# A 640-point forward transform split by residues modulo five, one slab at a time, with its output columns placed in order in PSUM

## The chip, the cores and the metric

The kernel runs on one core of one Trainium2 chip. The metric is device microseconds of one execution, the median of three runs. A core has five engines with a queue each: TensorE (PE in the profile, its weight loads PEld), VectorE (DVE), ScalarE (ACT), GpSimd (POOL) and SyncE (SP), which here issues all DMAs. Each queue runs its instructions in the order in which the program emits them, and an instruction waits until what it reads is written and what it overwrites has been read. SBUF is the working memory, PSUM (eight banks of 512 fp32 values per partition) is where TensorE writes.

## The reference, cut to what matters

`x` is 2048 x 640 in bf16. Two branches start from the same row-normalized `xn`: a spectral filter `s` and a gated feed-forward network `g`.

```python
xn = _layernorm(x, axis=-1)
X = jnp.fft.rfft2(xn, axes=(-2, -1)) * (w_r + 1j * w_i)      # 2048 x 321
s = jnp.fft.irfft2(X, s=(2048, 640), axes=(-2, -1))
g = _silu((_gelu(xn @ w_gate) * (xn @ w_up)) @ w_down)       # 640 -> 1536 -> 640
return x + s * g
```

## The kernel before

The 2048 rows are held as 16 *slabs* of 128 rows (row = 16 * partition + slab). Slabs 4g to 4g+3 form *group* g of the feed-forward network (FFN), 512 rows.

**The order of work** is one hand-written list, `back` (L787 to L801), of 144 *steps* of FFN work; `plan` (filled by `put(step, item)`) names what else is emitted directly after each step. So the order on every queue is fixed by this list: after a step's FFN instructions come its plan items, in the order of the `put` calls. Steps 3 to 15 are small FFN pieces of group 0; from step 16 an *FFN half* is five matmuls of 512 columns, for `w_gate` (even steps, `psg`, evicted by ScalarE's gelu at L726) or `w_up` (odd steps, `psu`, evicted by VectorE's product at L728 into `uT`). Steps 24 to 35 are the twelve thirds of group 0's down projection (eight matmuls of 320 columns each, L747), 36 to 59 the halves of group 1, 60 to 71 its down projection, 72 to 107 group 2, 108 to 143 group 3. `psg` and `psu` have two banks each.

**The spectral branch** lies between these steps.

- Normalization of a slab: statistics on VectorE (L182, L187), the root on POOL (`root`, L198), and either `norm` on VectorE (L204) or `norm_act` on ScalarE (L435, with `shift` on POOL for its bias).
- *Folds* on VectorE, for two slabs at once: `fold_a` (L444, L445) forms x[d] + x[d+320] and x[d] - x[d+320], `fold_b` (L453, L454) adds and subtracts mirrored halves of each. That splits the 640-point transform into four products of 160 inputs and up to 161 outputs.
- `slab_S1` (L483): the first factor of the 2048-point transform, five matmuls of 128 columns per slab into `pz`; ScalarE copies `pz` to SBUF (L485).
- `group_D` (L503): the 640-point products, for one slab and then five times three. `d_group` (L487) does 128 of the 160 inputs by L493 and the other 32, four row groups of the array side by side, by L497, for 161 columns each, into two PSUM tiles `pd`. Two copies (L509, two of the twelve on VectorE) interleave even and odd frequencies on their way to `zd` in SBUF, and SP stores `zd` to the DRAM scratch `ZDR`, two or four DMAs per group.
- `load_B2` reads `ZDR` back transposed (tile B, L534), `s2_in` and `s2_out` (L560 to L593) do the rest of the 2048-point transform and the filter, `UDR` and `load_V` turn it back.
- The inverse: `slab_S1i` (L639, copy L641), `group_Di` (`d_group` with the table `FI`, copies L664), `group_cs`, `group_Y` and `finish` on VectorE.

`pz`, `pd`, `px`, `pu` and `pv` all take turns in one ring of two PSUM tiles of two banks (`psB`, tag "b"); `group_D` and `group_Di` take both at once.

The step numbers of the stages: the forward stage is `F0 = 30` to `z_end` = 56; `s2` starts at `z_end + 9` = 65 and takes 24 steps, `load_V` comes at 89, the inverse starts at `vs0` = 97 with a new group of three slabs every 7.5 steps, its S1 at a, a+2 and a+4, its D at a+6.

`FT` and `FI` are the tables of the forward and the inverse 640-point products, made at the start: phases on ScalarE (`ft_v`), reduced on POOL (`ft_phase`), sines on ScalarE (`ft_sin`). GEN is one area of SBUF from which the tables' intermediate values are cut.

Of the kernel before, what the change touches and what calls it, by code (L numbers as in the profile page):

```python
# [76 lines left out]
def build(nc, env):  # L77
# [275 lines left out]

    mg = {}
# [80 lines left out]
        nc.scalar.activation(out=X[:, n1, :], in_=X[:, n1, :], func=ACT.Identity, scale=rstd[n1], bias=nmr[n1])  # L435
# [2 lines left out]
    uvs = {}

    def fold_a(pair):  # L440
        xn = X[:, 2 * pair:2 * pair + 2, :]
        assert ("n", 2 * pair + 1) in done
        uvs[pair] = uvt = work.tile([P, 2, D], BF16, tag="uv", bufs=2, name="uvt")
        nc.vector.tensor_tensor(out=uvt[:, :, 0:320], in0=xn[:, :, 0:320], in1=xn[:, :, 320:640], op=ALU.add)  # L444
        nc.vector.tensor_tensor(out=uvt[:, :, 320:640], in0=xn[:, :, 0:320], in1=xn[:, :, 320:640], op=ALU.subtract)  # L445

    def fold_b(pair):
        xf[pair] = f = work.tile([P, 2, D], BF16, tag="xf", bufs=2, name="f")
        s4 = uvs.pop(pair).rearrange("p k (t d) -> p k t d", t=2)
        dm = f[:, :, 0:512].rearrange("p k (g d) -> p k g d", g=4)  # L450
        dr = f[:, :, 512:640].rearrange("p k (g d) -> p k g d", g=4)
        for gs, op in ((slice(0, 4, 3), ALU.add), (slice(1, 3), ALU.subtract)):
            nc.vector.tensor_tensor(out=dm[:, :, gs, :], in0=s4[:, :, :, 32:160], in1=s4[:, :, :, 287:159:-1], op=op)  # L453
            nc.vector.tensor_tensor(out=dr[:, :, gs, :], in0=s4[:, :, :, 0:32], in1=s4[:, :, :, 319:287:-1], op=op)  # L454
# [22 lines left out]
    zbuf = fv.rearrange("p g l -> p (g l)").bitcast(BF16)[:, 0:4 * D].rearrange("p (s c k) -> p s c k", s=4, c=5)  # L477

    def slab_S1(n1):
        f = xf[n1 // 2]  # L480
        pz = psB.tile([P, 5, P], FP32, tag="b")
        for c in range(5):
            nc.tensor.matmul(pz[:, c, :], lhsT=chunk(f, n1 % 2, c), rhs=Tfwd[:, n1, :], start=True, stop=True)  # L483
# [1 line left out]
        nc.scalar.copy(out=Zt[n1], in_=pz)  # L485

# [10 lines left out]
                nc.tensor.matmul(out[a][g], lhsT=lhs[a][r, 4, :], rhs=T[r, 4, 0:w], start=False, stop=(a == n - 1))  # L497
# [4 lines left out]

    def group_D(i):  # L503
        n0, n = DF[i]
        pd = d_group([Zt.pop(n0 + a) for a in range(n)], FT, LH)
        zd = work.tile([P, 3, 2, LP], BF16, tag="zd", bufs=2, name="zd")[:, 0:n]
        for b in range(2):
            ev = nc.vector.tensor_copy if i in (2, 5) and b == 1 else nc.scalar.copy
            ev(out=zd.rearrange("p a c (m b) -> p a c m b", b=2)[:, :, :, :, b], in_=pd[b])  # L509
# [320 lines left out]
    put(17, stats, 8)  # L830
    put(19, stats, 9)
    put(23, fold_a, 0)
    for it in ((silu_table,), (tinv_sin, 0), (tinv_sin, 1), (ft_sin, 0)):
        put(23, *it)
    put(24, fold_b, 0)
    put(28, mg_mask)
    put(25, root, 8, 2)
    put(25, fold_a, 1)
    for q in range(4):
        put(24 + q, tfwd, q)  # L840
    put(27, norm, 8)
    put(28, fold_b, 1)
    put(29, stats, 10)
# [1 line left out]
    put(29, mg_sin)
    put(29, mg_build)
    put(31, norm, 9)
    put(32, stats, 11)
    put(33, root, 10, 2)
    put(34, norm, 10)  # L850
    put(35, norm, 11)
    put(38, stats, 12)
    put(41, stats, 13)
    put(41, root, 12, 2)
    put(42, stats, 14)
    put(43, norm, 12)
    put(44, norm, 13)
    put(44, stats, 15)
    put(45, root, 14, 2)
    put(46, norm, 14)  # L860
    put(47, norm, 15)
# [2 lines left out]
    for i, (n0, n) in enumerate(DF):
        a = F0 if i == 0 else F0 + 5 * i - 3
        for k in range(n):
            put(a + k, slab_S1, n0 + k)
        put(a + n, group_D, i)
    for pair in range(6):
        b = F0 + 3 * pair + (0 if pair < 4 else 3)  # L870
        put(b, fold_a, pair + 2)
        put(b + 1, fold_b, pair + 2)
    z_end = F0 + 26
# [88 lines left out]
```

## Time and profile before

| | us |
|---|---|
| median of three runs | 203.33 |
| lowest, highest | 203.01, 203.89 |
| the profiled execution, whole time | 203.86 |
| its span, first to last instruction | 201.7 |

| stretch of the span, us | what runs | PE busy | DVE busy | ACT busy | DMA share |
|---|---|---|---|---|---|
| 0.00 to 10.00 | start, slabs 0 and 1 | 8.27 | 7.77 | 3.71 | 0.87 |
| 26.70 to 35.40 | FFN halves 16 to 23 | 8.70 | 5.16 | 5.97 | 1.06 |
| 35.40 to 51.20 | steps 24 to 35 | 15.80 | 11.75 | 11.56 | 0.79 |
| 51.20 to 86.10 | steps 36 to 59 | 34.88 | 22.36 | 24.89 | 0.58 |
| 102.00 to 130.00 | steps 72 to 92, s2 | 28.00 | 15.60 | 21.19 | 0.31 |
| 150.60 to 183.00 | steps 108 to 131, inverse | 32.40 | 25.05 | 18.80 | 0.29 |

The first table's difference between whole time and span is what lies around the first and last instruction. The second is read across: an engine's busy time beside the length of the stretch. Rows of instructions further down read: start, duration (for several in a row, of all together), engine, line, operation, output <- input, shapes, count, and in square brackets how long the engine sat idle before and what released it. Rows of groups read: busy microseconds in all, mean nanoseconds of one, then the idle time before them and its releasers.

### The profile page before, as it was taken

What the parts mean: (1) busy time and instruction counts of PE and PEld (TensorE: products, weight loads), DVE (VectorE), ACT (ScalarE), POOL (GpSimd) and SP (SyncE); (2) the same over time, 40 slices, a digit from 0 to 9 for tenths busy, and PEclk for the clock granted to TensorE, in tenths of its full rate; (3) what the DMA queues carried; (4) which work ended last, traced back from release to release, by engine and by line L of the source; (5) the groups of instructions that cost most, each with busy time, mean ns of one, the idle gap of its engine ahead of it and who ended that gap; (6) DMA issues with size and microseconds to landing.
All of it is one profiled execution on the core that took longest, in us unless ns stands there. A gap on an engine that the chain in (4) does not pass through costs nothing.

```text
span 201.7 us, 4218 instructions
## 1 busy us (share of the span) xinstructions
PE 196.1 (97%) x1581; PEld 119.5 (59%) x1581; DVE 128.0 (63%) x339; ACT 122.7 (61%) x210; POOL 34.3 (17%) x61
## 2 busy tenths in 40 slices
PE   7899999999999999999999999999999999999993
PEld 5678854777555555576634334456775555556772
DVE  7786866677398972435566476223358776867673
ACT  2457657966886777414887878324475647476632
POOL 4327869972201100000000000000000000000000
PEclk9999999999999999999999999999999999999999
DMA  6999999958566647339844202389301343224312
GB/s 164 307 301 283 356 344 195 144 103 301 116 170 153 159 115 300 116 94 301 237 134 132 92 25 81 130 199 328 129 0 67 99 111 120 69 94 142 89 67 63
DMA packets 40163, 32.43 MB, mean 161 GB/s; under 512 B 14928, under 2 KB 38096, under 8 KB 39888
## 3 DMA queue, kind: packets, MB, share of 16 engines
q1 hardware_dynamic: 40144, 32.17, 56.9%
q8 instruction: 12, 0.20, 0.4%
q14 instruction: 7, 0.06, 0.1%
HBM read 19.03 MB, written 7.88 MB: 133 GB/s over the span
## 4 chain that ended last, share of the span: by engine, by line
PE 89%; DMA 4%; DVE 3%; SPq 1%; POOL 1%; issue 1%; ACT 0%
PE psu L722 24%; PE psg L722 24%; PE psg L747 13%; PE psu L747 13%; PE pd L493 5%; PE pv L639 2%; DMA Vin<-UDR 2%; PE pz L483 2%; PE pu L587 2%; DMA X<-in_A_x_dram 2%; PE pd L497 2%; PE px L560 2%; DVE st L182 1%; SPq L610 1%; POOL rst L198 1%
## 5 line engine op out<-in xcount | busy, mean ns | idle before, releaser
L722 PE MATMUL psu<-xnT,Wu 128*128 128x512 bf16 (+2 forms) x295 | 61.5, 340 | 0.3
L722 PE MATMUL psg<-xnT,Wg 128*128 128x512 bf16 (+2 forms) x295 | 61.4, 340 | 0.0
L728 DVE TENSOR_TENSOR uT<-psu,ge 128x512 bf16<-128x512 f32 (+2 forms) x59 | 34.3, 584 | 30.1 <-PE psu L722 22.5
L726 ACT ACTIVATE ge<-psg 128x512 bf16<-128x512 f32 (+2 forms) x59 | 30.5, 518 | 27.8 <-PE psg L722 25.9
L747 PEld LDWEIGHTS <-uT 128*128 128x128 bf16 x396 | 37.1, 98 | 14.3 <-issue 0.6
L722 PEld LDWEIGHTS <-Wu 128*128 128x128 bf16 x295 | 26.6, 98 | 23.1 <-issue 2.9
L722 PEld LDWEIGHTS <-Wg 128*128 128x128 bf16 x295 | 26.7, 98 | 21.8 <-issue 1.4
L747 PE MATMUL psg<-Wd,uT 128*128 128x320 bf16 (+1 forms) x204 | 30.4, 294 | 0.0
L747 PE MATMUL psu<-Wd,uT 128*128 128x320 bf16 (+1 forms) x192 | 29.2, 296 | 0.0
L572 DVE TENSOR_TENSOR X<-xs,W 128x972 bf16<-128x972 bf16 (+2 forms) x22 | 13.3, 648 | 10.2 <-ACT xs L568 10.2
L641 ACT CAST W<-pv 128x640 bf16<-128x640 f32 x16 | 11.1, 692 | 6.0 <-PE pv L639 6.0
L182 DVE BATCH_NORM_STATS2 st<-X 128x6 f32<-128x320 bf16 x32 | 14.2, 481 | 0.2 <-DMA X<-in_A_x_dram 0.2
L509 ACT CAST zd<-pd 128x966 bf16<-128x966 f32 (+1 forms) x10 | 10.5, 1103 | 5.3 <-PE pd L497 5.3
L664 ACT ACTIVATE W<-pd 128x960 bf16<-128x960 f32 (+2 forms) x14 | 10.1, 780 | 5.0 <-PE pd L497 5.0
L485 ACT CAST GEN<-pz 128x640 bf16<-128x640 f32 x16 | 11.0, 696 | 3.2 <-PE pz L483 3.2
L593 ACT CAST X<-pu 128x486 bf16<-128x486 f32 (+4 forms) x22 | 12.3, 558 | 0.4
L568 ACT CAST xs<-px 128x972 bf16<-128x972 f32 (+2 forms) x11 | 10.3, 937 | 2.1 <-PE px L560 2.1
L198 POOL TENSOR_TENSOR rst<-ve,mhalf 128x1 f32<-128x1 f32 (+2 forms) x9 | 6.5, 719 | 26.8 <-DVE ve L196 26.8
L670 DVE TENSOR_TENSOR W<-W 128x960 bf16<-128x960 bf16 (+1 forms) x12 | 6.8, 599 | 4.8 <-ACT W L664 4.8
L697 DVE TENSOR_TENSOR Yall<-Yall,G 128x640 bf16<-128x640 bf16 (+3 forms) x19 | 8.2, 434 | 1.6 <-ACT G L752 1.3
L756 DVE SCALAR_TENSOR_TENSOR G<-th,psu 128x320 bf16<-128x320 f32 x8 | 3.9, 488 | 8.2 <-ACT th L755 8.2
L698 DVE TENSOR_TENSOR Yall<-Yall,xt 128x640 bf16<-128x640 bf16 (+3 forms) x19 | 8.3, 439 | 0.7
(132 smaller groups left out, 197.4 us busy)
## 6 DMA issues: line engine op xcount, KB each, us to landing
W<-W SPq DMA_DIRECT2D x4, 642.0 KB, 4.2
xt<-in_A_x_dram SPq DMA_DIRECT2D x8, 320.0 KB, 3.8
ZDR<-zd SPq DMA_DIRECT2D x20, 120.4 KB, 3.2
UDR<-X SPq DMA_DIRECT2D x10, 240.8 KB, 2.2
out_dram<-Yall SPq DMA_DIRECT2D x14, 160.0 KB, 1.9
B<-ZDR SPq DMA_DIRECT2D x8, 240.8 KB, 3.9
W<-UDR SPq DMA_DIRECT2D x4, 481.5 KB, 7.3
X<-in_A_x_dram SPq DMA_DIRECT2D x3, 640.0 KB, 7.6
```

What stands on the lines that cost most here:

```text
L182: nc.vector.bn_stats(out=st[:, k, :], in_=X[:, n1, 320 * k:320 * k + 320])
L485: nc.scalar.copy(out=Zt[n1], in_=pz)
L509: ev(out=zd.rearrange("p a c (m b) -> p a c m b", b=2)[:, :, :, :, b], in_=pd[b])
L568: nc.scalar.copy(out=xs, in_=px[:, :, 0:n * w].rearrange("p k (h l) -> p k h l", l=w))
L572: nc.vector.tensor_tensor(out=pp[-1], in0=xs, in1=WT[:, :, h0:h0 + n, l0:l0 + w], op=ALU.mult)
L593: nc.scalar.copy(out=us[:, :, :, c0:c0 + (w + 1 - m) // 2], in_=pv[:, :, :, m:w:2])
L641: nc.scalar.copy(out=vs, in_=pv)
L664: nc.scalar.activation(out=eo[:, b, :, a0:a1].rearrange("p k a n -> p a k n"), in_=py[b][:, a0:a1], func=ACT.Copy, scale=(2.0 if silu[a0] ...
L722: nc.tensor.matmul(ps, lhsT=WT[:, c, t * P:(t + 1) * P], rhs=xnT[g][:, c, c0:c1_], start=(c == 0), stop=(c == 4))
L726: nc.scalar.activation(out=ges[t], in_=ps, func=ACT.Gelu_apprx_tanh)
L728: nc.vector.tensor_tensor(out=uT[g][:, t, c0:c1_], in0=ps, in1=ges[t], op=ALU.mult)
L747: nc.tensor.matmul(ph, lhsT=uT[g][:, t, j * P:(j + 1) * P], rhs=Wd[:, t, c0:c1_], start=(t == 0), stop=(t == NT - 1))
```

## The change

The 640-point forward product is split by the frequency's residue modulo five. The frequencies that are multiples of five need only the sum of the five blocks of 128 inputs (`fold_y`, result `y0`). For all others one block can be subtracted from the rest (`fold_x`), which leaves 512 inputs; `fold_a` and `fold_b` fold these by mirror images into four groups of 128. So every product has exactly 128 rows and there is no remainder of 32: `slab_D` does four matmuls of 128 columns and two of 65 for one slab, and `group_D` is gone for the forward stage. `l_cols` places each matmul's output columns at their frequency's own place in PSUM: steps of 2 and gaps for the four groups, steps of 5 for the multiples of five. One ScalarE copy of 2 x 321 dense columns per slab follows, and two stores to `ZDR` per slab (32 instead of 22).

The folds work on four slabs at once, nine VectorE instructions, in a scratch area of GEN that the tables' intermediate values use before. `FT` shrinks to 130 columns a group with other phases, taken from two new integer tables (`meo`, two more POOL operations). `norm` of slabs 12 to 15 becomes `norm_act` on ScalarE, at steps 46 and 47. The forward stage gets a list of places, `FA`, one per slab: S1 at `FA[n]`, D one step later. `z_end` moves from step 56 to 60, the start of s2 from 65 to 67, `load_V` from 89 to 91, `vs0` from 97 to 99; the inverse groups start 6.7 instead of 7.5 steps apart. `load_xt` uses the "xf" buffers, since "uv" is gone. Some table work is placed a step earlier or some steps later.

```diff
-    FT = consts.tile([P, 5, LH], BF16)
+    FT = consts.tile([P, 5, 130], BF16)
...
+    meo = gtile([2, P], INT32)
+    nc.gpsimd.iota(meo[:, 0].rearrange("p (q r) -> p q r", r=4), pattern=[[5, 32], [1, 4]], base=1,
+                   channel_multiplier=0)
+    nc.gpsimd.iota(meo[:, 1].rearrange("p (q h i) -> p q h i", h=2, i=2), pattern=[[5, 32], [3, 2], [1, 2]], base=0,
+                   channel_multiplier=0)
+    scr = goff[0]
+    ftm = gtile([5, LH], FP32)
...
-        a_m = affine("a_m", pf, 4.0, 130.0)
-        b_2 = affine("b_2", pf, 2.0, 385.0)
-        b_3 = affine("b_3", pf, 2.0, 65.0)
-        a_r = affine("a_r", s_f, 4.0, 2.0)
-        s21 = affine("s21", s_f, 2.0, 1.0)
-        b_r = fma("b_r", times("hs", s21, 1.0, hi_f), 1.0, cq)
+        a_m = affine("a_m", pf, 4.0, 2.0)
+        b_2 = affine("b_2", pf, 2.0, 321.0)
+        b_3 = affine("b_3", pf, 2.0, 1.0)
+        a_y = affine("a_y", pf, 10.0, 5.0)
         kc.append(cq)
-        ab.extend([(a_m, b_0), (a_m, b_1), (a_m, b_2), (a_m, b_3), (a_r, b_r)])
+        ab.extend([(a_m, b_0), (a_m, b_1), (a_m, b_2), (a_m, b_3), (a_y, None)])
 
...
     def ft_v(g):
-        nc.scalar.activation(out=fv[:, g, :], in_=lint, func=ACT.Identity, scale=ab[g][0], bias=ab[g][1])
+        if g < 5:
+            parts = [(0, P, meo[:, g // 2])] if g < 4 else [(0, 65, lint[:, 0:65]), (65, 130, lint[:, 0:65])]
+        else:
+            parts = [(0, LH, lint)]
+        for k, (c0, c1_, m) in enumerate(parts):
+            nc.scalar.activation(out=fv[:, g, c0:c1_], in_=m, func=ACT.Identity, scale=ab[g][0],
+                                 bias=(b_0, b_1)[k] if g == 4 else ab[g][1])
+
+    FW = (130, LH)
+    nc.gpsimd.memset(fv[:, 0:4, P:130], 0.0)
 
...
+    y0s = {}
+
+    def scratch(o, n, w):
+        return GEN[:, scr + o:scr + o + n * w // 2].bitcast(BF16).rearrange("p (s d) -> p s d", s=n)
+
+    def slabs(n0, n):
+        assert all(("n", n0 + k) in done for k in range(n))
+        return X[:, n0:n0 + n, :]
+
+    def fold_y(n0, n, k):
+        xn = slabs(n0, n)
+        t = scratch(2304, n, 256)
+        if k == 0:
+            nc.vector.tensor_tensor(out=t, in0=xn[:, :, 0:256], in1=xn[:, :, 256:512], op=ALU.add)
+            return
+        if k == 1:
+            y = work.tile([P, 4, P], BF16, tag="y0", bufs=2, name="y0")
+            for a in range(n):
+                y0s[n0 + a] = y[:, a, :]
+            y0s[n0, n] = y = y[:, 0:n, :]
+            nc.vector.tensor_tensor(out=y, in0=t[:, :, 0:P], in1=t[:, :, P:256], op=ALU.add)
+            return
+        y = y0s[n0, n]
+        nc.vector.tensor_tensor(out=y, in0=y, in1=xn[:, :, 512:640], op=ALU.add)
+
+    def fold_x(n0, n, k):
+        xn = slabs(n0, n)
+        xp = scratch(0, n, D)
+
+        def blocks(t):
+            return t.rearrange("p s (t e) -> p s t e", e=64)
+
+        def outer(t):
+            return t.rearrange("p s (t b e) -> p t s b e", b=2, e=64)[:, 0:5:2]
+
+        ref = blocks(xn)[:, :, 2:8:5, :]
+        if k == 0:
+            nc.vector.tensor_tensor(out=outer(xp), in0=outer(xn),
+                                    in1=ref.unsqueeze(1).to_broadcast([P, 3, n, 2, 64]), op=ALU.subtract)
+        else:
+            nc.vector.tensor_tensor(out=blocks(xp)[:, :, 6:2:-3, :], in0=blocks(xn)[:, :, 6:2:-3, :], in1=ref,
+                                    op=ALU.subtract)
+
+    def fold_a(n0, n, k):
+        xp, uvt = scratch(0, n, D), scratch(1280, n, 512)
+        lo = xp[:, :, 0:384].rearrange("p s (t e) -> p s t e", e=192)[:, :, :, 0:P]
+        hi = xp[:, :, 256:640].rearrange("p s (t e) -> p s t e", e=192)[:, :, :, 64:192]
+        nc.vector.tensor_tensor(out=uvt[:, :, 256 * k:256 * k + 256].rearrange("p s (t e) -> p s t e", e=P),
+                                in0=lo, in1=hi, op=(ALU.add, ALU.subtract)[k])
+
+    def fold_b(n0, n, k):
+        if k == 0:
+            f = work.tile([P, 4, 512], BF16, tag="xf", bufs=2, name="f")
+            for a in range(n):
+                xf[n0 + a] = f[:, a, :]
+            xf[n0, n] = f[:, 0:n, :]
+        s4 = scratch(1280, n, 512).rearrange("p s (w d) -> p s w d", w=2)
+        dm = xf[n0, n].rearrange("p k (g d) -> p k g d", g=4)
+        gs, op = ((slice(0, 4, 3), ALU.add), (slice(1, 3), ALU.subtract))[k]
+        nc.vector.tensor_tensor(out=dm[:, :, gs, :], in0=s4[:, :, :, 0:P], in1=s4[:, :, :, 255:127:-1], op=op)
+
+    def chunk(n1, c):
+        return xf[n1][:, c * P:(c + 1) * P] if c < 4 else y0s[n1]
 
...
-        f = xf[n1 // 2]
         pz = psB.tile([P, 5, P], FP32, tag="b")
         for c in range(5):
-            nc.tensor.matmul(pz[:, c, :], lhsT=chunk(f, n1 % 2, c), rhs=Tfwd[:, n1, :], start=True, stop=True)
+            nc.tensor.matmul(pz[:, c, :], lhsT=chunk(n1, c), rhs=Tfwd[:, n1, :], start=True, stop=True)
...
-    def group_D(i):
-        n0, n = DF[i]
-        pd = d_group([Zt.pop(n0 + a) for a in range(n)], FT, LH)
-        zd = work.tile([P, 3, 2, LP], BF16, tag="zd", bufs=2, name="zd")[:, 0:n]
-        for b in range(2):
-            ev = nc.vector.tensor_copy if i in (2, 5) and b == 1 else nc.scalar.copy
-            ev(out=zd.rearrange("p a c (m b) -> p a c m b", b=2)[:, :, :, :, b], in_=pd[b])
+    def l_cols(bank, g):
+        if g == 4:
+            return bank[:, 0:325].rearrange("p (m e) -> p m e", e=5)[:, :, 0]
+        v = bank[:, 0:320].rearrange("p (q e) -> p q e", e=10)
+        if g < 2:
+            return v[:, :, 2:10:2]
+        return bass.AP(v.tensor, v.offset + 1, [list(v.ap[0]), list(v.ap[1]), [6, 2], [2, 2]])
+
+    def slab_D(n1):
+        z = Zt.pop(n1)
+        pd = psB.tile([P, 2, 512], FP32, tag="b", name="pd")
+        for g in range(4):
+            nc.tensor.matmul(l_cols(pd[:, g % 2], g), lhsT=z[:, g, :], rhs=FT[:, g, 0:P], start=True, stop=True)
+        for c in range(2):
+            nc.tensor.matmul(l_cols(pd[:, c], 4), lhsT=z[:, 4, :], rhs=FT[:, 4, 65 * c:65 * c + 65],
+                             start=True, stop=True)
+        zd = work.tile([P, 2, LP], BF16, tag="zd", bufs=4, name="zd")[:, :, 0:L]
+        nc.scalar.copy(out=zd, in_=pd[:, :, 0:L])
         for a in range(2):
-            if n == 1:
-                nc.sync.dma_start(out=ZDR[a, :, n0].rearrange("c p l -> p c l"), in_=zd[a:P:2, 0, :, 0:L])
-            else:
-                for c in range(2):
-                    nc.sync.dma_start(out=ZDR[a, c, n0:n0 + n].rearrange("n p l -> p n l"),
-                                      in_=zd[a:P:2, :, c, 0:L])
+            nc.sync.dma_start(out=ZDR[a, :, n1].rearrange("c p l -> p c l"), in_=zd[a:P:2])
 
...
+        t = work.tile([P, 4, 512], BF16, tag="xf", bufs=2, name="xt")
+        t = t.rearrange("p a b -> p (a b)")[:, 0:2 * D].rearrange("p (a d) -> p a d", a=2)
...
+    for at, *items in (
+            (17, (stats, 8)), (18, (stats, 9)), (20, (stats, 10)), (22, (stats, 11), (root, 8, 4)),
+            (24, (fold_x, 0, 4, 0), (fold_x, 0, 4, 1)), (25, (fold_a, 0, 4, 0), (fold_a, 0, 4, 1)),
+            (26, (fold_b, 0, 4, 0), (fold_b, 0, 4, 1)), (27, (fold_y, 0, 4, 0), (fold_y, 0, 4, 1), (fold_y, 0, 4, 2)),
+            (28, (norm, 8)), (29, (fold_x, 4, 4, 0), (fold_x, 4, 4, 1)), (30, (fold_a, 4, 4, 0)),
+            (31, (fold_a, 4, 4, 1), (fold_b, 4, 4, 0)), (32, (fold_b, 4, 4, 1), (fold_y, 4, 4, 0)),
+            (33, (fold_y, 4, 4, 1), (fold_y, 4, 4, 2), (norm, 9)), (34, (norm, 10), (norm, 11)), (35, (stats, 12)),
+            (36, (stats, 13)), (37, (fold_x, 8, 4, 0)), (38, (fold_x, 8, 4, 1), (fold_a, 8, 4, 0)),
+            (39, (fold_a, 8, 4, 1)), (40, (fold_b, 8, 4, 0), (fold_b, 8, 4, 1)), (41, (fold_y, 8, 4, 0)),
+            (42, (fold_y, 8, 4, 1), (fold_y, 8, 4, 2), (half_stats, 14, 0)), (43, (half_stats, 14, 1)),
+            (44, (stats, 15), (root, 12, 4), (shift, 12, 4)), (46, (norm_act, 12), (norm_act, 13)),
+            (47, (norm_act, 14), (norm_act, 15)), (48, (fold_x, 12, 4, 0), (fold_x, 12, 4, 1)),
+            (49, (fold_a, 12, 4, 0)), (50, (fold_a, 12, 4, 1), (fold_b, 12, 4, 0)), (51, (fold_b, 12, 4, 1)),
+            (52, (fold_y, 12, 4, 0), (fold_y, 12, 4, 1)), (53, (fold_y, 12, 4, 2))):
+        for it in items:
+            put(at, *it)
...
+    FA = (30, 32, 33, 35, 37, 39, 40, 42, 44, 46, 48, 50, 54, 55, 57, 58)
+    for n1 in range(NS):
+        put(FA[n1] + 1, slab_D, n1)
+        put(FA[n1], slab_S1, n1)
+    z_end = F0 + 30
...
-    sb = z_end + 9
+    sb = z_end + 7
...
-    for i, at in enumerate((vs0 - 1, vs0, vs0 + 6, vs0 + 16, vs0 + 25)):
+    for i, at in enumerate((vs0 - 1, vs0, vs0 + 5, vs0 + 14, vs0 + 22)):
...
-        a = vs0 + 15 * i // 2
+        a = vs0 + 67 * i // 10
...
-            put(min(d + (5 + k if n == 3 else 2), vs0 + 44), finish, n0 + k)
+            put(min(d + (5 + k if n == 3 else 2), vs0 + 41), finish, n0 + k)
```

More of the change, by code (lines that the diff above doesn't have):

```diff
@@ L335, in build @@
     fv = gtile([10, LH], FP32)
-    ftm = gtile([5, LH], FP32)
     def ft_v(g):
-        nc.scalar.activation(out=fv[:, g, :], in_=lint, func=ACT.Identity, scale=ab[g][0], bias=ab[g][1])
+        if g < 5:
[7 more added lines that the diff above has]
+    nc.gpsimd.memset(fv[:, 0:4, P:130], 0.0)
     def ft_phase(t, k):
-        v = fv[:, 5 * t:5 * t + 5, :]
+        v = fv[:, 5 * t:5 * t + 5, 0:FW[t]]
+        fm = ftm[:, :, 0:FW[t]]
         if k == 0:
-            nc.gpsimd.tensor_scalar(out=ftm, in0=v, scalar1=1.0 / 1280.0, scalar2=MAGIC, op0=ALU.mult, op1=ALU.add)
+            nc.gpsimd.tensor_scalar(out=fm, in0=v, scalar1=1.0 / 1280.0, scalar2=MAGIC, op0=ALU.mult, op1=ALU.add)
         elif k == 1:
-            nc.gpsimd.tensor_scalar(out=ftm, in0=ftm, scalar1=MAGIC, scalar2=-1280.0, op0=ALU.subtract, op1=ALU.mult)
+            nc.gpsimd.tensor_scalar(out=fm, in0=fm, scalar1=MAGIC, scalar2=-1280.0, op0=ALU.subtract, op1=ALU.mult)
         else:
-            nc.gpsimd.tensor_tensor(out=v, in0=v, in1=ftm, op=ALU.add)
+            nc.gpsimd.tensor_tensor(out=v, in0=v, in1=fm, op=ALU.add)
     def ft_sin(t):
-        nc.scalar.activation(out=(FT, FI)[t], in_=fv[:, 5 * t:5 * t + 5, :], func=ACT.Sin,
+        nc.scalar.activation(out=(FT, FI)[t][:, :, 0:FW[t]], in_=fv[:, 5 * t:5 * t + 5, 0:FW[t]], func=ACT.Sin,
                              scale=TWO_PI / 1280.0 * (1.0 - 2e-7))
@@ L436, in norm_act @@
         done.add(("n", n1))
[L438 to L454, printed above, removed]
@@ L456, in chunk @@
-    def chunk(f, k, c):
-        return f[:, k, c * P:(c + 1) * P]
+    y0s = {}
[19 more added lines that the diff above has]
+        nc.vector.tensor_tensor(out=y, in0=y, in1=xn[:, :, 512:640], op=ALU.add)
@@ L498, in d_group @@
         return [t[:, :, 0:n * w].rearrange("p k (a m) -> p a k m", a=n) for t in ps]
-    DF = [(0, 1)] + [(n0, 3) for n0 in range(1, NS, 3)]
     DG = [(n0, min(3, NS - n0)) for n0 in range(0, NS, 3)]
-    def group_D(i):
-        n0, n = DF[i]
-        pd = d_group([Zt.pop(n0 + a) for a in range(n)], FT, LH)
-        zd = work.tile([P, 3, 2, LP], BF16, tag="zd", bufs=2, name="zd")[:, 0:n]
-        for b in range(2):
-            ev = nc.vector.tensor_copy if i in (2, 5) and b == 1 else nc.scalar.copy
-            ev(out=zd.rearrange("p a c (m b) -> p a c m b", b=2)[:, :, :, :, b], in_=pd[b])
-        for a in range(2):
-            if n == 1:
-                nc.sync.dma_start(out=ZDR[a, :, n0].rearrange("c p l -> p c l"), in_=zd[a:P:2, 0, :, 0:L])
-            else:
-                for c in range(2):
-                    nc.sync.dma_start(out=ZDR[a, c, n0:n0 + n].rearrange("n p l -> p n l"),
-                                      in_=zd[a:P:2, :, c, 0:L])
+    def l_cols(bank, g):
[15 more added lines that the diff above has]
+        nc.scalar.copy(out=zd, in_=pd[:, :, 0:L])
+        for a in range(2):
+            nc.sync.dma_start(out=ZDR[a, :, n1].rearrange("c p l -> p c l"), in_=zd[a:P:2])
     warm_bank = []
@@ L628, in load_xt @@
     def load_xt(pair):
-        t = work.tile([P, 2, D], BF16, tag="uv", bufs=2, name="xt")
+        t = work.tile([P, 4, 512], BF16, tag="xf", bufs=2, name="xt")
+        t = t.rearrange("p a b -> p (a b)")[:, 0:2 * D].rearrange("p (a d) -> p a d", a=2)
         for a in range(2):
@@ L822, in build @@
         put(13, ft_phase, 1, k)
-    for it in (mg_iota, mg_phase1, mg_phase2):
-        put(13, it)
     put(12, tinv_mask, 0)
@@ L829, in build @@
         put(17 + 2 * k, slab_T, 4 + k, 2)
-    put(17, stats, 8)
-    put(19, stats, 9)
-    put(23, fold_a, 0)
+    put(23, mg_iota)
+    put(23, mg_phase1)
+    put(23, mg_phase2)
     for it in ((silu_table,), (tinv_sin, 0), (tinv_sin, 1), (ft_sin, 0)):
[L834 to L838, printed above, removed]
+        put(22, *it)
     for q in range(4):
[L840 to L843, printed above, removed]
+        put(23 + q, tfwd, q)
@@ L844, in build @@
     put(28, ft_sin, 1)
[L845 to L861, printed above, removed]
+    put(30, mg_mask)
+    put(31, mg_sin)
+    put(31, mg_build)
+    for at, *items in (
[14 more added lines that the diff above has]
+            put(at, *it)
@@ L862, in build @@
     F0 = 30
     TURN = 45
[L864 to L873, printed above, removed]
+    FA = (30, 32, 33, 35, 37, 39, 40, 42, 44, 46, 48, 50, 54, 55, 57, 58)
+    for n1 in range(NS):
+        put(FA[n1] + 1, slab_D, n1)
+        put(FA[n1], slab_S1, n1)
@@ L874, in build @@
+    z_end = F0 + 30
     for k in range(4):
-        put(32 + 3 * k, slab_T, 8 + k, 2)
+        put(34 + 3 * k, slab_T, 8 + k, 2)
         put(65 + 3 * k, slab_T, 12 + k, 2)
@@ L912, in build @@
         for k in range(n):
-            put(min(d + (5 + k if n == 3 else 2), vs0 + 44), finish, n0 + k)
+            put(min(d + (5 + k if n == 3 else 2), vs0 + 41), finish, n0 + k)
             if (n0 + k) % 2 and 1 < (n0 + k + 3) // 2 < 8:
-                put(min(d + (5 + k if n == 3 else 2), vs0 + 44), load_xt, (n0 + k + 3) // 2)
+                put(min(d + (5 + k if n == 3 else 2), vs0 + 41), load_xt, (n0 + k + 3) // 2)
     warm_pe(19)
```

## Prediction

> **What bounds the kernel now.** I read the busy table first, then the chain of waits, then TensorE and ScalarE in order of time, and last the groups with shapes kept apart.
>
> ```profile
> span 201.7 us, 4218 instructions
> PE 196.1 (97%) x1581; PEld 119.5 (59%) x1581; DVE 128.0 (63%) x339; ACT 122.7 (61%) x210; POOL 34.3 (17%) x61
> PE 89%; DMA 4%; DVE 3%; SPq 1%; POOL 1%; issue 1%; ACT 0%
> ```
>
> TensorE is the bound: 97% busy, 89% of the chain. So a microsecond of matmuls removed is one gained, and one in which TensorE waits for another engine is one lost, wherever it falls.
>
> TensorE around a forward group of three slabs:
>
> ```profile
> 48.57 0.44 PE L483 MATMUL pz<-Tfwd,f 128*128 128x128 bf16 x5
> 48.85 1.25 PE L747 MATMUL psu<-Wd,uT 128*128 128x320 bf16 x8
> 49.94 1.02 PE L493 MATMUL pd<-FT,GEN 128*128 128x161 bf16 x12
> 50.90 0.39 PE L497 MATMUL pd<-FT,GEN 32*128 32x161 bf16 x12
> 51.22 1.25 PE L722 MATMUL psg<-xnT,Wg 128*128 128x512 bf16 x5
> ```
>
> Durations of pipelined matmuls overlap, so I take differences of starts: a slab's first product (S1) 0.28 us, eight down-projection matmuls 1.09, a group's second product (D) 51.22 - 49.94 = 1.28; an FFN half is 1.08.
>
> **Part 1, TensorE's own work.** Removed: the six D groups before. By the same differences they hold 0.56 (one slab), 1.28 four times and 1.46 once (0.18 of it a wait): 7.14 us. Added: per slab four matmuls of 128 columns and two of 65, each on 128 rows. The trace has no matmul whose output columns lie apart in PSUM. Lower bound, the dense S1 rows: 0.28/5 = 0.056 for 128 columns, so 0.28 to 0.34 a slab (the short pair between column pace, 0.03, and 0.056), 4.5 to 5.4 us in all, a gain of 1.7 to 2.6. Upper bound, the slowest column pace of any matmul here, the warm-up at the start:
>
> ```profile
> 1.17 4.23 PE L524 MATMUL psg<-GEN 128*128 128x256 bf16 x19 [1.17 <-DVE negpi L212]
> ```
>
> (4.23 - 0.42 for the last)/18 = 0.212 for 256 columns, 0.107 for 128 and 0.054 for 65: 0.54 a slab, 8.6 us, a loss of 1.4. Between these I go by how fast PSUM is seen to move single elements:
>
> ```profile
> L568 ACT CAST xs<-px 128x972 bf16<-128x972 f32 x5 | 4.8, 966 | 1.1 <-PE px L560 1.1
> L568 ACT CAST xs<-px 128x642 bf16<-128x642 f32 x1 | 0.7, 695 | 0.0
> L485 ACT CAST GEN<-pz 128x640 bf16<-128x640 f32 x16 | 11.0, 696 | 3.2 <-PE pz L483 3.2
> L509 ACT CAST zd<-pd 128x966 bf16<-128x966 f32 x8 | 9.6, 1248 | 4.8 <-PE pd L497 4.8
> ```
>
> ScalarE reads PSUM one element after another at (966 - 695)/330 = 0.82 ns each; only a dense matmul goes at half of that, 0.42 ns a column, as if neighbours went in pairs. A step of two leaves one of each pair. And the one write with a step of two here (L509, 1248 ns against 966 for as many dense elements) is the dearer. So I take the upper bound: **+1.4 us**.
>
> The Trainium skill (PSUM — Partial Sum Buffer, Specifications) says that PSUM has lines of 8 bytes and that any pattern that is not contiguous slows matmuls significantly. It gives no figure; by it the dense price above is out, and the sum stays on the side taken here. No run shown so far has such an output.
>
> **Part 2, a wait for ScalarE in step 47.** Four normalizations (slabs 12 to 15) move from VectorE to ScalarE's queue. ScalarE's rows in order of time:
>
> ```profile
> 28.14 0.92 ACT L435 ACTIVATE X<-X,nmr,rst 128x640 bf16<-128x640 bf16 x1 [1.53 <-POOL nmr L430]
> 28.96 0.58 ACT L726 ACTIVATE ge<-psg 128x512 bf16<-128x512 f32 x1
> 29.44 0.91 ACT L435 ACTIVATE X<-X,nmr,rst 128x640 bf16<-128x640 bf16 x1
> 47.74 0.69 ACT L485 CAST GEN<-pz 128x640 bf16<-128x640 f32 x1 [0.68 <-PE pz L483]
> 48.33 0.44 ACT L752 ACTIVATE G<-psg 128x320 bf16<-128x320 f32 x1
> ```
>
> Start to start: normalization 0.82, gelu 0.49, copy of pz 0.59 (its result is taken up 0.72 after its start); ScalarE starts 0.20 after TensorE is through (an FFN half ends at 61.20, its gelu starts at 61.40). After step 46's FFN half (time 0) ScalarE's order is gelu, norm 12, norm 13, copy pz(9), norm 14, norm 15, copy pd(9), gelu. Copy pz(9) lands at 0.20 + 0.49 + 1.64 + 0.72 = 3.05. TensorE has S1(9) 0.28 and step 47's half 1.08, and wants D(9) at 1.36: it stands **1.7 us**. The next D meets the same backlog: copy pz(10) lands at 6.36, TensorE is there at 6.03: **0.3**. Behind D(9) stands every later FFN matmul, so nothing covers this. At five places where slabs follow in neighbouring steps (2, 6, 12, 13, 15) the copy of pd stands ahead of that of pz: 0.20 + 0.59 + 0.72 = 1.51 against S1 and a step, 1.37: 0.15 each, **0.75** (slab 12: the last fold instead). Before, one D of this stage waited, 0.18.
>
> **Part 3, the inverse stage.** Its groups start 6.7 instead of 7.5 steps apart, so group 1's first S1 now comes directly behind group 0's D, and group 4's behind group 3's. S1 needs a bank pair that D has just filled. Before, an FFN half lies between:
>
> ```profile
> 165.67 0.39 PE L497 MATMUL pd<-FI,W 32*128 32x160 bf16 x12
> 165.99 1.25 PE L722 MATMUL psu<-xnT,Wu 128*128 128x512 bf16 x5
> 167.11 0.38 PE L639 MATMUL pv<-Tinv,W 128*128 128x128 bf16 x4
> 166.09 1.83 ACT L664 ACTIVATE W<-pd 128x960 bf16<-128x960 f32 x2 [0.57 <-PE pd L497]
> ```
>
> D ends at 165.99, ScalarE's first copy lands at 167.06, S1 starts at 167.11, 1.12 later and 0.04 after the half was through. Without the half all 1.1 is a wait: twice, **2.2 us**.
>
> **Part 4, covered edits.** VectorE's folds: two-input rows cost 0.07 us + 1/1920 us per element (640 in 0.41, 512 in 0.34, 128 in 0.135). Before, four slabs take 24 - 12 = 12 instructions, 3.54 us; after, nine with 8192 elements, 4.9: 5.4 us more in all. Four norms (0.36 each) and two copies (1.2 each) go away: net +1.6 in a stage where VectorE is busy 22.4 of 34.9 us; a uT multiply may be four FFN halves late before its bank is wanted. The first fold waits for the sine that reads the scratch area's old contents (L329, until 38.5) and ends near 42.2; S1(0) comes at 42.8. The two statistics moved ahead (2.1 us) fit where VectorE is busy 5.2 of 8.7 us (26.7 to 35.4). Copies of pd: 16 of 0.70, 11.1 us for 13.0. Ten more ZDR stores, 0.6 us each on SP's queue: 6 us over some 45 that have 30 issued; behind them stand only transposes wanted in step 72. POOL's tables (7.2 us of small operations) start 3 us later, for use in step 67. At the start the chain goes through the load of slab 1 (landing at 5.95), ahead of which the shorter constants only add idle time. Reading B: before, D(15) had 10.9 us to the first px; now eight thirds, 8.7, for copy 0.9, second store 0.65, landing as before 3.3 (85.0 to 88.3), load up to 4.2 (88.3 to 92.5): 0 to 0.4 us of wait, taken as **0.2**; by the slowest load, 5.7, 1.9.
>
> **Sum.** +1.4 + 1.7 + 0.3 + 0.75 - 0 + 2.2 + 0.2 = +6.6 us (the 0.18 is in the 7.14). The profiled execution took 203.86, 2.16 around its span and 0.53 over the median 203.33; added to the median: **209.9 us**.
>
> **Rivals.**
> *Dense pace.* The step costs TensorE nothing: -2.2 in place of +1.4 (middle of its bounds), the waits a little longer (D comes earlier, +0.5). For it: in these rows the array, not PSUM, sets a dense matmul's pace. Against it: the pairs above. 203.3 + 6.6 - 3.6 + 0.5 = 206.8.
> *Saved columns decide (the other side).* At dense pace D saves up to 2.6; if ScalarE's backlog and the inverse waits together stay under 1.6 us, the kernel gains over 0.5%: 200.7 with none, 202.3 at that point. For it: only TensorE bounds. Against it: the orders of the queues, which leave over 4 us of waits by rows with little spread.
> *VectorE becomes the bound.* If broadcast and five-dimensional folds lose the pace of two elements per cycle, each four slabs take 4.3 us more: S1(0) waits 3.7, S1(4k) again, 214 or more. Against it: the reversed L453 keeps the pace.
> *B late.* The 1.9 instead of 0.2: 211.6.
> *It doesn't do what it says:* no; the issued TensorE instructions are the six per slab.
>
> **How the numbers follow.** Forecast 0.50, dense pace 0.30, other side 0.12 (half of it within 0.5%, about what a measurement can tell from no change), VectorE 0.03, B late 0.05. The forecast's own range, with waits off by a quarter, is 208.3 to 211.3. The 8-in-10 range reaches down through the dense case, its waits off by half as well (206.8 - 1.8 = 205.0), and up to B late: 205.0 to 211.7; outside lie the other side and VectorE. Faster 0.07, same 0.06, slower 0.87.
>
> **What would show it.** Part 1: starts of neighbouring D matmuls, 0.107 apart (rival: 0.056). Part 2: TensorE idle before D(9) for 1.7 us, released by ScalarE's copy of pz, with two normalizations just ahead of it. Part 3: two gaps of 1.1 us before a pv, released by L664's successor. No TensorE wait for VectorE at S1(0). It is wrong if TensorE's idle time between 35 and 190 us stays under 2 us, or D is dense.

## The result, and the profile after

| | before | after |
|---|---|---|
| median, us | 203.33 | 212.12 |
| lowest to highest, us | 203.01 to 203.89 | 211.99 to 212.20 |
| span of the profiled execution, us | 201.7 | 210.4 |
| step 36 starts at | 51.22 | 53.40 |
| step 60 starts at | 85.93 | 92.80 |

The ratio is 1.043 (95% interval 1.041 to 1.045): 8.8 us slower, where +6.6 was forecast; 212.12 lies 0.4 us over the top of the range. Step 24 starts at 35.2 us in both; by the starts of the stages, 2.2 us came in steps 24 to 35, 4.7 in steps 36 to 59 and 1.8 behind step 60.

The busy table after, and then TensorE's waits (engine, line and its releaser; total us, times, longest):

```profile
span 210.4 us, 4156 instructions
PE 198.0 (94%) x1534; PEld 121.9 (58%) x1549; DVE 131.1 (62%) x318; ACT 126.3 (60%) x221; POOL 38.1 (18%) x64
```

```profile
PE pd L570 <- ACT GEN L541: 3.4, 2, 1.8
PE pv L701 <- ACT W L726: 2.1, 2, 1.1
```

TensorE's busy share fell from 97 to 94%. Two D's wait for ScalarE's copy of `pz`, two S1's of the inverse for ScalarE's copy of `pd`; the table of before has neither line. One of the four I had not foreseen. TensorE after, from D(0), the second product of slab 0, to D(1):

```profile
44.37 0.60 PE L570 MATMUL pd<-FT,GEN 128*128 128x128 bf16 x4
44.76 0.32 PE L572 MATMUL pd<-FT,GEN 128*128 128x65 bf16 x2
44.89 1.28 PE L809 MATMUL psu<-Wd,uT 128*128 128x320 bf16 x8
46.00 0.39 PE L539 MATMUL pz<-Tfwd,f 128*128 128x128 bf16 x4
46.23 0.22 PE L539 MATMUL pz<-Tfwd,y 128*128 128x128 bf16 x1
46.28 1.25 PE L809 MATMUL psg<-Wd,uT 128*128 128x320 bf16 x8
49.37 0.61 PE L570 MATMUL pd<-FT,GEN 128*128 128x128 bf16 x4 [1.84 <-ACT GEN L541]
```

One D takes 44.89 - 44.37 = 0.52 us: 0.10 for 128 strided columns. D(1) should start at 46.28 + 1.09 = 47.37 and starts at 49.37. Its releaser is the copy of `pz(1)`, so ScalarE in order of time:

```profile
44.12 0.45 ACT L814 ACTIVATE G<-psg 128x320 bf16<-128x320 f32 x1
47.41 0.40 ACT L417 ACTIVATE sg<-vg,negpi 128x128 f32<-128x128 int32 x1 [2.85 <-DVE vg L413]
47.72 0.68 ACT L575 CAST zd<-pd 128x642 bf16<-128x642 f32 x1
48.30 0.44 ACT L814 ACTIVATE G<-psu 128x320 bf16<-128x320 f32 x1
48.62 0.69 ACT L541 CAST GEN<-pz 128x640 bf16<-128x640 f32 x1
```

ScalarE itself was idle for 2.85 us, with three finished PSUM results behind the instruction it stood at: the sine `mg_sin`. It belongs to a small table, `MG`, that is made in four steps: phases on POOL (`mg_phase1`, `mg_phase2`), a mask on VectorE (`mg_mask`), the sine on ScalarE, and the build on POOL (`mg_build`). The sine's releaser on VectorE, with the first and the last fold ahead of it, and some rows of POOL:

```profile
37.58 0.96 DVE L489 TENSOR_TENSOR GEN<-X 128x1536 bf16<-128x1536 bf16 x1 [1.28 <-ACT Tinv L334]
44.29 0.42 DVE L492 TENSOR_TENSOR GEN<-X 128x512 bf16<-128x512 bf16 x1
47.15 0.23 DVE L413 TENSOR_SCALAR vg<-vg 128x128 int32<-128x128 int32 x1 [2.44 <-POOL vg L374]
```

```profile
35.78 1.04 POOL L198 TENSOR_TENSOR rst<-ve,mhalf 128x4 f32<-128x4 f32 x1 [2.14 <-DVE ve L196]
36.78 0.14 POOL L378 IOTA kr<- 128x16 int32 x1
37.52 0.19 POOL L374 TENSOR_SCALAR cs<-pb 128x1 f32<-128x1 f32 x1
37.82 1.11 POOL L374 TENSOR_SCALAR php<-pb,zc 128x1 f32<-128x1 f32 x1
43.19 1.60 POOL L374 TENSOR_SCALAR vg<-kr,n1x,php 128x16 int32<-128x16 int32 x1
44.77 0.36 POOL L374 TENSOR_SCALAR vg<-kr,n1x,phs 128x16 int32<-128x16 int32 x1
46.75 0.36 POOL L374 TENSOR_SCALAR vg<-kr,n1x,phs 128x16 int32<-128x16 int32 x1
```

The same chain on POOL in the kernel before, again some rows:

```profile
33.59 0.14 POOL L364 IOTA kr<- 128x16 int32 x1
34.62 0.27 POOL L360 TENSOR_SCALAR php<-pb,zc 128x1 f32<-128x1 f32 x1
38.20 0.92 POOL L360 TENSOR_SCALAR vg<-kr,n1x,phm 128x16 int32<-128x16 int32 x1
40.43 0.36 POOL L360 TENSOR_SCALAR vg<-kr,n1x,phs 128x16 int32<-128x16 int32 x1
```

POOL's phases run from 36.78 to 47.1, 10.3 us, instead of 33.59 to 40.8 before. They start later, since the root for slabs 8 to 11 (L198) stands ahead of them; and single operations take 1.1 to 1.6 us that take 0.27 and 0.36 elsewhere. VectorE's folds run from 37.58 to 44.7; from then to 47.15 VectorE is idle, and the same operations take 0.36.

The second late D, first on TensorE, then on ScalarE:

```profile
70.70 1.24 PE L784 MATMUL psu<-xnT,Wu 128*128 128x512 bf16 x5
73.47 0.61 PE L570 MATMUL pd<-FT,GEN 128*128 128x128 bf16 x4 [1.53 <-ACT GEN L541]
```

```profile
70.62 0.60 ACT L788 ACTIVATE ge<-psg 128x512 bf16<-128x512 f32 x1 [0.34 <-PE psg L784]
71.11 1.72 ACT L449 ACTIVATE X<-X,nmr,rst 128x640 bf16<-128x640 bf16 x2
72.74 0.68 ACT L541 CAST GEN<-pz 128x640 bf16<-128x640 f32 x1
73.31 1.74 ACT L449 ACTIVATE X<-X,nmr,rst 128x640 bf16<-128x640 bf16 x2
```

D(9) is wanted at 70.70 + 1.08 = 71.78 and starts 1.69 later, behind two normalizations. The inverse, where S1 stands directly behind D (TensorE):

```profile
153.85 0.39 PE L553 MATMUL pd<-FI,W 32*128 32x160 bf16 x12
155.29 0.38 PE L701 MATMUL pv<-Tinv,Vin 128*128 128x128 bf16 x4 [1.06 <-ACT W L726]
```

### The profile page after: what moved, and what is told of

Same layout as the page of the kernel before. It is cut to its first block, busy times and chain, and to the rows that moved or that the text cites. A ratio compares the mean times of both kernels' runs of the same rounds, so it can differ in the third digit from the quotient of the medians.

```text
span 210.4 us, 4156 instructions
## 1 busy us (share of the span) xinstructions
PE 198.0 (94%) x1534; PEld 121.9 (58%) x1549; DVE 131.1 (62%) x318; ACT 126.3 (60%) x221; POOL 38.1 (18%) x64
## 4 chain that ended last, share of the span: by engine, by line
PE 65%; ACT 3%; issue 1%; DVE 0%; DMA 0%
PE psu L784 16%; PE psg L784 16%; PE psg L809 10%; PE psu L809 9%; PE pv L701 2%; PE pd L570 2%; PE pd L549 2%; PE pu L648 2%; PE px L621 2%; PE pz L539 2%; ACT X L449 1%; ACT W L726 1%; PE pd L553 1%; ACT GEN L541 1%; PE pd L572 0%
## 5 line engine op out<-in xcount | busy, mean ns | idle before, releaser
L784 PE MATMUL psg<-xnT,Wg 128*128 128x512 bf16 (+2 forms) x286 | 60.4, 339 | 0.7 <-ACT xnT L845 0.2
L575 ACT CAST zd<-pd 128x642 bf16<-128x642 f32 x16 | 11.1, 695 | 7.3 <-PE pd L572 4.6
L570 PE MATMUL pd<-FT,GEN 128*128 128x128 bf16 x64 | 9.7, 306 | 3.8 <-ACT GEN L541 3.4
L629 ACT CAST xs<-px 128x972 bf16<-128x972 f32 (+2 forms) x11 | 10.3, 938 | 2.9 <-PE px L621 2.9
L818 DVE SCALAR_TENSOR_TENSOR G<-th,psg 128x320 bf16<-128x320 f32 x8 | 3.9, 488 | 12.3 <-ACT th L817 12.3
L570 PEld LDWEIGHTS <-GEN 128*128 128x128 bf16 x64 | 5.5, 118 | 9.5 <-ACT GEN L541 9.3
L198 POOL TENSOR_TENSOR rst<-ve,mhalf 128x1 f32<-128x1 f32 (+1 forms) x7 | 5.4, 765 | 26.4 <-DVE ve L196 26.4
```

What stands on the lines that cost most here:

```text
L570: nc.tensor.matmul(l_cols(pd[:, g % 2], g), lhsT=z[:, g, :], rhs=FT[:, g, 0:P], start=True, stop=True)
L575: nc.scalar.copy(out=zd, in_=pd[:, :, 0:L])
L784: nc.tensor.matmul(ps, lhsT=WT[:, c, t * P:(t + 1) * P], rhs=xnT[g][:, c, c0:c1_], start=(c == 0), stop=(c == 4))
```

## The experiments

Each is an edit of the changed kernel (212.12 us). Ratios are to the kernel before, with their 95% interval in brackets. The kernel before took 203.0 to 203.1 us beside these runs and 203.33 beside the 212.12, so what a run gives back is good to about 0.3 us.

### The POOL chain

Phases early (POOL's steps back to 13):

```diff
-    put(23, mg_iota)
-    put(23, mg_phase1)
-    put(23, mg_phase2)
+    for it in (mg_iota, mg_phase1, mg_phase2):
+        put(13, it)
```

> The three POOL steps that make mg's phases go back to step 13, ahead of the power for slabs 8 to 11; all else as in the changed kernel (212.1 us). Theory: D(1)'s wait of 1.84 us is the end of a chain POOL phases, VectorE mask (L413), ScalarE sine (L417), copy of pd, copy of pz; phases that start at 33.6 instead of 36.8 us end before ScalarE reaches the sine, and the wait goes: 210.3 us. If POOL's small operations are slowed by VectorE's folds beside them, the phases now take about 7.2 us instead of 10.3, since most of them run before the first fold at 37.6. Rival: the copies that stand behind the sine are late without it (gelu, copy of pd, copy of pz in one queue), and under 0.6 us comes back: above 211.5 us; phases still 10 us if it is their place and not the folds.

210.90 us, ratio 1.038 (1.036 to 1.039): 1.2 us back, between the two. The wait of D(1) fell to 0.56. Some rows of POOL, then VectorE's first fold and its norm of slab 8, show why the phases were still long:

```profile
37.13 0.37 POOL L374 TENSOR_SCALAR vg<-kr,n1x,phm 128x16 int32<-128x16 int32 x1
37.47 1.44 POOL L374 TENSOR_SCALAR vg<-kr,n1x,phs 128x16 int32<-128x16 int32 x1
43.14 1.03 POOL L198 TENSOR_TENSOR rst<-ve,mhalf 128x4 f32<-128x4 f32 x1
```

```profile
37.45 0.96 DVE L489 TENSOR_TENSOR GEN<-X 128x1536 bf16<-128x1536 bf16 x1 [1.28 <-ACT Tinv L334]
44.20 0.45 DVE L204 TENSOR_SCALAR X<-X,mva,rst 128x640 bf16<-128x640 bf16 x1 [1.10 <-POOL rst L198]
```

Two instructions of the same line and shape, one before the first fold and one from its start on, 0.37 against 1.44 us. Five of the eight `vg` fell into the folds, so the phases took 9.7 us (33.47 to 43.19), not 7.2. And what was late next moved: now the root for slabs 8 to 11 stands behind the slow operations, VectorE's norm of slab 8 waits 1.10 us for it, and the mask behind that norm is late.

Mask, sine and build four steps later, phases left where they are:

```diff
-    put(30, mg_mask)
-    put(31, mg_sin)
-    put(31, mg_build)
+    put(34, mg_mask)
+    put(35, mg_sin)
+    put(35, mg_build)
```

> POOL's phases stay where the changed kernel has them; only what follows them moves back: mask from step 30 to 34, sine and build from step 31 to 35, behind D(0), D(1) and D(2) on ScalarE's queue (212.1 us otherwise). Theory: the phases may be as late and as slow as they are, what cost time was ScalarE waiting for them with the copies behind: the wait of 1.84 us at D(1) goes wholly, 0.6 us more than with the phases moved early (where mask and sine still stood ahead of the copies and 0.56 us stayed): 210.3 us or a little less. VectorE no longer idles 2.4 us for POOL at the mask, so folds lie beside POOL's table products, which take 0.7 to 1.4 us each instead of 0.36. Rival: the tables, now 4 us later still, hold up their transposes at step 45 or the sine's place in step 35 stalls as it did in step 31: above 211.5 us.

210.57 us (1.038, 1.036 to 1.039): 1.55 us back. D(1) follows its neighbour without a wait (47.33 after 46.24 + 1.09), while the phases, with folds beside most of them, now take 13.6 us (36.73 to 50.3). So the price lay in what ScalarE's queue held behind the sine, not in POOL's time. About 0.3 of the 1.84 us is lost again elsewhere: D(3), which did not wait in the changed kernel, waits 0.20.

### Normalization on VectorE

```diff
-    (46, (norm_act, 12), (norm_act, 13)), (47, (norm_act, 14), (norm_act, 15)),
+    (46, (norm, 12), (norm, 13)), (47, (norm, 14), (norm, 15)),
```

> Slabs 12 to 15 are normalized on VectorE again (norm instead of norm_act, same steps 46 and 47); all else as in the changed kernel (212.1 us). Theory: the four normalizations ahead of the copy of pz(9) are the waits of D(9) and D(10), 1.53 + 0.16 and 0.29 us; both go: 210.1 us. Rival: VectorE's four norms (0.36 us each) push folds and products behind them, and the wait goes over to S1(12) or to an FFN bank: gain under 1 us, above 211.1 us.

210.36 us (1.036, 1.034 to 1.037): 1.76 back. D(9) and D(10) start within 0.08 us of the FFN half ahead, S1(12) too. Both waits were those of the four normalizations.

### The inverse's spacing

```diff
-        a = vs0 + 67 * i // 10
+        a = vs0 + 7 * i
```

> Inverse groups start every 7 steps instead of every 6.7, so an FFN half lies between each D and the next group's first S1; all else as in the changed kernel (212.1 us). Theory: the two waits of pv at 155.3 and 184.5 (1.06 and 1.05 us) go, and the last group, two steps later, still ends under the last FFN halves: 210.0 us. Rival: the end is set by the last finish instructions, which come up to two steps later: 211.0 us or more.

210.08 us (1.034, 1.032 to 1.036): 2.04 back. Both waits of `pv`, 2.1 us in the trace, are gone, so the later last group costs hardly anything.

### The output columns

Dense columns, in another order:

```diff
     def l_cols(bank, g):
...
+        c0 = g // 2 * P
+        return bank[:, c0:c0 + (65 if g == 4 else P)]
```

> slab_D writes each product's columns side by side in PSUM (0 to 127, 128 to 255, 256 to 320) instead of each at its frequency's place; so the frequencies reach the filter in another order, and the output isn't the reference's. Instructions and bytes are the same. Theory: the step of two is what makes 128 columns take 0.10 us; dense ones take 0.056, a slab 0.28 to 0.34 instead of 0.52, and 16 slabs give back 2.9 to 3.8 us, less what ScalarE's waits grow (0.5): 208.3 to 209.7 us. Rival: the pace comes from elsewhere (the weight loads, the table's columns), starts stay 0.10 apart and the time within 0.4 us of 212.1.

Two of four executions, the profiled one among them, took 209.1 us at a granted clock of 1.0, the other two 210.7 at 0.992; the median is 209.88 (1.033, 1.029 to 1.037). A slab's D takes 0.28 us instead of 0.52. That is 3.8 us of TensorE's work in 16 slabs, of which 3.0 is seen at the full clock: D comes earlier and stands longer behind the same copies (by differences of starts D(1) 2.26 for 2.00, D(10) 0.55 for 0.29).

Runs of 33 neighbours, put in order by the copy (`FT` gets 132 columns a group in the order of the runs):

```diff
-        v = bank[:, 0:320].rearrange("p (q e) -> p q e", e=10)
+        v = bank[:, 0:330].rearrange("p (r q) -> p r q", q=33)
...
-            return v[:, :, 2:10:2]
+            return v[:, 2:10:2, :]
...
-        nc.scalar.copy(out=zd, in_=pd[:, :, 0:L])
+        nc.scalar.copy(out=zd.rearrange("p c (q r) -> p c q r", r=10),
+                       in_=pd[:, :, 0:330].rearrange("p c (r q) -> p c q r", q=33))
```

> The same frequencies, in blocks: each matmul writes runs of 33 neighbouring columns (frequency 10q + r lies at 33r + q), 132 and 66 columns instead of 128 and 65, and ScalarE's copy of pd puts them in order, reading PSUM in steps of 33 values. All else as in the changed kernel (212.1 us). Theory: a run of 33 neighbours goes at dense pace, a slab in 0.29 instead of 0.52 us, and ScalarE's reads cost the same in any step (L654 reads in steps of two: 486 elements in 574 ns, the line of dense ones): the copy stays at 0.71 us, and the time goes to 209 to 209.7 us as with dense columns. Rival: steps in PSUM cost ScalarE what they cost TensorE: the copy takes 1.2 us or more, the copies of pz behind it come 0.5 us later at each slab, and most or all is given back: above 211 us.

209.29 us (1.031, 1.029 to 1.032). TensorE from one D to the end of the FFN half behind it, and ScalarE's two copies as groups:

```profile
53.85 0.41 PE L572 MATMUL pd<-FT,GEN 128*128 128x132 bf16 x4
54.09 0.23 PE L574 MATMUL pd<-FT,GEN 128*128 128x66 bf16 x2
54.15 1.24 PE L788 MATMUL psu<-xnT,Wu 128*128 128x512 bf16 x5
55.23 0.39 PE L541 MATMUL pz<-Tfwd,f 128*128 128x128 bf16 x4
```

```profile
L577 ACT CAST zd<-pd 128x660 bf16<-128x660 f32 x16 | 11.3, 706 | 5.0 <-PE pd L574 3.1 <-ACT GEN L543 1.8
L543 ACT CAST GEN<-pz 128x640 bf16<-128x640 f32 x16 | 11.1, 694 | 2.5 <-PE pz L541 2.5
```

660 columns in 0.30 us, where 642 strided ones took 0.52. The copy that reads PSUM in steps of 33 values costs 706 ns for 660 elements beside 694 for 640 dense ones: nothing for the step. Here the order can be had on ScalarE's side free of charge.

### Together

The three repairs (mask and sine late, norms on VectorE, spacing 7), columns as changed:

> Mask, sine and build as in the run before, normalizations of slabs 12 to 15 on VectorE, inverse groups every 7 steps; the strided output columns stay. Theory: the three waits are separate and add: 212.1 - 1.84 - 1.76 - 2.04 = 206.5 us; what is left over the kernel before is D's own work (16 times 0.52 against 6.96 us without its wait: 1.4) and waits of 0.2 us at several slabs. Rival: the waits hide one another, and under 4.5 us comes back: above 207.6 us.

206.39 us (1.016, 1.015 to 1.018): 5.7 us back, where the three runs alone gave 1.55 + 1.76 + 2.04 = 5.35. None of the waits hides another; they add.

The three repairs and the runs of 33:

> The three repairs and the blocks of 33 together. Theory: 206.5 - 16 times 0.23 = 202.8 us, up to 203.3 with waits that grow, so level with the kernel before (203.1) or a little faster. Rival: with the waits gone, ScalarE's backlog in the forward stage decides and half of the gain stays out: 204.5 us or more.

203.11 us, ratio 1.0004 (0.9995 to 1.0013): level with the kernel before. What remained were waits of D for its `pz`, so D moved a step away from its S1:

```diff
-    FA = (30, 32, 33, 35, 37, 39, 40, 42, 44, 46, 48, 50, 54, 55, 57, 58)
+    FA = (30, 32, 33, 35, 37, 39, 40, 42, 44, 46, 48, 50, 54, 55, 56, 57)
...
-        put(FA[n1] + 1, slab_D, n1)
+        put(FA[n1] + 2, slab_D, n1)
```

> As the run with the three repairs and the blocks of 33 (203.1 us), with each D two steps behind its S1 instead of one, and slabs 14 and 15 one step earlier (S1 at 56 and 57), so that the last D stays in step 59. Theory: what is left are the waits of D for the copy of pz when S1 lies only one FFN half before and a copy of pd stands ahead of it: by differences of starts 0.20, 0.21, 0.35, 0.38, 0.20 and 0.38 us at slabs 2, 3, 4, 6, 13 and 15, 1.7 us in all. With a step more each copy has landed: 201.4 us, 0.8% faster than the kernel before. Rival: D directly ahead of the next S1 puts two ring tiles into use in one place, S1 waits for the copy of the pd before it, and less than 0.7 us comes back: above 202.4 us.

200.98 us, ratio 0.9895 (0.988 to 0.991), 2.1 us faster than with one step and 1% faster than the kernel before. The busy table of this run:

```profile
span 199.2 us, 4151 instructions
PE 193.0 (97%) x1534; PEld 119.1 (60%) x1549; DVE 131.9 (66%) x320; ACT 122.5 (62%) x217; POOL 38.4 (19%) x63
```

TensorE is at 97% again, with less to do than before, and its table of waits has no line for `pd` or `pv` any more.

The same with the strided columns:

> The same places with the strided output columns of the changed kernel (three repairs, no blocks; 206.4 us with D one step behind). Theory: the small waits there are 0.17, 0.20, 0.10, 0.23, 0.19 and 0.19 us, 1.1 in all: 205.3 us, and against the run beside it the strided columns cost 16 times 0.52 - 0.30 = 3.5 us by themselves, with no wait mixed in: 3.3 to 4 us. Rival: a D that is longer leaves ScalarE more time, so that the step more brings nothing here: 206.0 us or more.

204.81 us (1.0086, 1.0067 to 1.0105). With all those waits gone the changed kernel's columns are still 1.8 us slower than the kernel before; against the run beside it the strided columns alone cost 3.83 us, 0.24 a slab. With the waits gone, the columns alone decide the sign.

## Why the prediction was right in direction and too small

*Part 1, held.* A slab's D takes 0.52 us from its start to that of the next matmul, and the matmuls behind it then take 0.03 us longer than elsewhere. TensorE after, the FFN half behind D(3):

```profile
55.00 1.27 PE L784 MATMUL psu<-xnT,Wu 128*128 128x512 bf16 x5
56.11 0.39 PE L539 MATMUL pz<-Tfwd,f 128*128 128x128 bf16 x4
```

From start to start that is 1.11 us; behind the runs of 33 the same half took 1.08 (54.15 to 55.23). So a slab costs 0.55 us where 0.54 was forecast, and 16 times 0.55 - 7.14 = +1.7 us for +1.4; the run with strided columns and no waits gives +1.8. The upper bound was the right choice, and the runs of 33 bear out the reason given, that neighbours must lie side by side. The bound's own figure, 0.107, is partly luck: it was taken from warm-up matmuls whose output columns do lie side by side, so they are slow for another reason, which stays open. What carries over is the argument of the pairs, half the dense pace (twice 0.056 us). One supporting argument was weak: a step makes ScalarE's write to SBUF dearer (L509), but its read of PSUM in steps of 33 costs nothing, so single elements are not dear to ScalarE as such.

The Trainium skill (PSUM — Partial Sum Buffer, Specifications) says that any pattern that is not contiguous slows matmuls significantly. The trace agrees for steps of two and more (0.10 against 0.056 us for 128 columns). It does not for the runs of 33: they have gaps between them and go at the dense pace, and the measurement decides.

*Part 2, held.* D(9) 1.69 us for 1.7, D(10) 0.29 for 0.3; slabs 2, 6, 13 and 15 waited 0.18, 0.23, 0.18 and 0.19, slab 12 not at all: 0.78 for 0.75.

*Part 3, held.* The two waits of `pv` are 1.06 + 1.05 = 2.1 us for 2.2.

*Part 4, one item failed.* Reading B cost nothing (0.2 forecast), stores and copies stayed covered. The folds of four slabs took 5.5 us (37.58 to 43.07) instead of 4.9, and S1(0) waited 0.19 us for the last of them. The step that failed is "POOL's tables (7.2 us of small operations) start 3 us later, for use in step 67". Both halves were wrong. The first user is not step 67 but a mask in VectorE's queue after step 30 and a sine in ScalarE's after step 31, and ScalarE's queue holds the copies that the next D needs. (The change moves POOL's phases from step 13 to 23, the mask from 28 to 30 and the sine from 29 to 31.) And 7.2 us was carried over from a place with fewer folds beside it: here they took 10.3. The trace of before had the hint: `vg` at L360 took 0.57 to 0.92 us while folds ran and 0.37 after. The item was priced at nothing; it cost 1.84 us in the trace (2.0 by the starts), and 1.55 came back when the sine was moved. Without it the kernel takes 210.57, inside the range.

The sum by measured terms: 1.7 + 1.7 + 0.3 + 0.8 + 2.1 + 0 = 6.6, what was forecast. With D(1)'s 2.0, S1(0)'s 0.19 and gaps of 0.07 to 0.08 ahead of D(7), D(8) and D(11) it makes 9.0, against 8.8 measured; behind step 60 only 1.8 us was lost, less than the two waits of `pv` there.

Two bounds of the prediction do not follow from its own numbers. A quarter of its waits (5.15 us) is 1.3, so the forecast's own range would be 208.6 to 211.2; half of the dense case's waits is 2.8, which would put the lower end at 204.0. The upper end, which was passed, is not touched by either.

*Rivals.* Dense pace and VectorE as the bound did not come about, nor did B come late. "Saved columns decide" is false for the kernel as changed, but its mechanism is real: at dense pace and without the waits, with each D moved a step, the split is worth 2 us (200.98 against 203.03).

## What to carry to other kernels

An edit that delays small work on an idle engine is covered only if its first consumer is: follow it through every in-order queue it passes (here POOL, VectorE, ScalarE) and ask what stands behind it there, not when the last result is used. When a layout can be made by the engine that writes PSUM or by the one that reads it, price both; here ScalarE's read did it free and TensorE's write paid 3.8 us. And take a duration for a moved operation from a place that has the same neighbours beside it.

## What the hardware showed that I had not expected

POOL's operations on 128 x 16 values take 0.36 us alone and 0.6 to 1.9 us while VectorE adds or subtracts two SBUF operands (L489, L499, L511, L465, L472, L475), in the changed kernel and in both runs that move the table's steps; beside the folds of the kernel before they took 0.57 to 0.92. VectorE's pairs of folds (L499, L511) take 1.29 to 1.34 us beside them and 1.28 with POOL idle (at 77.35 us), so nearly the whole price is POOL's. The Trainium skill (SBUF — State Buffer, Who interferes with whom) says that a VectorE instruction with two SBUF inputs contends with a GpSimd instruction that reads SBUF, by an exclusive lock; the traces agree with the contention, and no run here shows the lock itself.

The dense columns ran in two of four executions at a granted clock of 0.992 (210.7 instead of 209.1 us), while the runs of 33, with nearly the same TensorE work, stayed at 1.0 in all four. Why is open.
